# Token mixing over 576 tokens: five tiles of 116 and 112 rows, or four of 128 and a stacked rest of 64

## The chip, the cores and the metric

The program runs on one core of a Trainium2 chip. The core has five engines with a queue of instructions each: PE (TensorE: matmuls and transposes), DVE (VectorE), ACT (ScalarE), POOL (GpSimd) and SP (SyncE), which here issues all loads and stores. Sixteen DMA engines move the data. The metric is device time in microseconds (us), less is better.

## The reference

Three layers follow each other on 4 batches of 576 tokens with 512 channels.

```python
# 1 attention with 8 heads of 64: tokens averaged by 4 (out_up), plus a band |i-j| < 4 (out_local)
attn_out = out_up + out_local
# 2 mixer
xt = x.transpose(0, 2, 1)
h = np.maximum(xt @ w_tok1, 0.0) @ w_tok2        # w_tok1 576x256, w_tok2 256x576
u = x + h.transpose(0, 2, 1)
x = u + np.maximum(u @ w_ch1, 0.0) @ w_ch2       # 512x1536, 1536x512
# 3 four experts of causal attention (head size 64), the best two of a gate weighted and summed
```

The weights of the mixer are float64 in the reference's inputs, so they reach the chip as pairs of 32-bit words and are turned into float32 there.

## The kernel before

**Numbers in two parts.** Products that need float32 accuracy are made from a high and a low part of each operand: `split` writes the high part with ACT and the low part (source minus high) with DVE, and `mm3` adds three matmuls for each pair of tiles, high by high, high by low and low by high.

**First stage, to about 256 us of the profile.** There are 16 units (b, p), one for each batch and pair of heads. `load_qk` and `load_v` issue a unit's loads. `scores` makes the band's scores `sl` and the averaged scores `sd` on PE, their maxima `nmx` and `nd` on DVE, the exponentials `P` (10 instructions) and `Pd` (4) on ACT, the reciprocal sums `rs` and `rd` on DVE, and the products with them on POOL. `turns` transposes them on PE (`pdt` from `Pd`, `tl` from `P`) and ACT copies the results to `PdT` and `PT`. `values` multiplies by the values (`pod`, `ol`) and DVE adds both into `U` (the tile `u`). After each half batch (two units) come three steps of token mixing: `tok_turn` transposes `U` into tiles of tokens (`tx`) and splits them (`xh`, `xl`); `tok_first` multiplies them by the first weight (`h`) and splits the rectified result (`h1h`, `h1l`); `tok_second` multiplies by the second weight (`pu`) and adds to `U`. There are eight half batches. The tokens lie in five tiles, `TS = [116, 116, 116, 116, 112]`.

**The weights.** `tok_weights` loads the first weight in three pieces, `wt_0` and `wt_2` (two tiles of 116 rows each) and `wt_4` (112 rows), then the second in four (`wt_00` to `wt_11`). For each piece `load_f32` puts the load on SP's queue, then two ACT, three DVE and one POOL instruction (`wt_t`, `wt_g`, `wt_a`, `wt_f`), and `split` follows. The order of the first loads is set by `START = 'q0 q1 q2 v0 w v1 v2'`: the token weights come behind the first unit's values. In the same way `convert` turns the channel weights (`wc`, 24 pieces of 512 KB); six of them are turned during the first stage. The raw pieces share two buffers.

**The order of the instructions** on each engine is not the order of the code: a scheduler with a timeline of its own puts them in a row at build time, by priorities (`PRI`, `ahead`) and by what it takes to be ready. Each engine then works through its row strictly, so an instruction that waits holds all behind it. PSUM has four tiles of one bank (`b1`, for `pdt`, `tl`, `pod`, `ol`, `tx`, `h`, `pu`) and two of two banks (`b2`, shared by `sl` and `sd`).

**Second and third stage.** The channel mixing (`c`, some 275 us of PE at work) and the experts (`proj`, `s`, `pt`, `o`, `wo`) follow.

Of the kernel before, what the change touches and what calls it, by code (L numbers as in the profile page):

```python
# [7 lines left out]
F32 = mybir.dt.float32  # L8
F32R = mybir.dt.float32r
# [3 lines left out]
AF = mybir.ActivationFunctionType  # L13
# [3 lines left out]
B, H, S, D = 4, 8, 576, 64  # L17
DM = H * D
NP = 4
TQ = 116  # L20
NT = 5
TS = [TQ, TQ, TQ, TQ, S - 4 * TQ]
WIN, WQ, NW = 64, 58, 10
KS = [min(max(WQ * w - 3, 0), S - WIN) for w in range(NW)]
SD = S // 4
# [2 lines left out]
DT = 256  # L28
# [38 lines left out]
def body(ctx, tc, qT, kT, vw, vp, wt1, wt2, wc1, wc2, wq, wk, wvg, wo, out):  # L67
    nc = tc.nc

    def pool(name, side=None, space=None, stack=ctx):  # L70
        kw = {"side": side} if side else {}
        if space is not None:
            kw["space"] = space
        return stack.enter_context(tc.tile_pool(name=name, bufs=1, reuse_waits="tile", **kw))
# [23 lines left out]
    def behind(ins):  # L98

        if order["on"]:  # L100
            tc.add_manual_dep(ins.ins, order["last"].ins.name,
                              mybir.DependencyInfo(mybir.DependencyClass.NoSync, mybir.DependencyReason.DATA),
                              reason="order")
        order["last"] = ins

    def mm(*a, **kw):
        behind(nc.tensor.matmul(*a, **kw))  # L107

    def tp(*a):
        behind(nc.tensor.transpose(*a))  # L110

    cst = pool("cst")
    ident = cst.tile([128, 128], F32, name="ident")
# [10 lines left out]
    for hf in range(2):  # L124
        m = band[WIN * hf:WIN * hf + WIN]
# [13 lines left out]
    U = [UA[:, :, b * S:(b + 1) * S] for b in range(B)]  # L139

    def split(hi, lo, src, relu=False, scale=None):
        nc.scalar.activation(hi, src, AF.Relu if relu else AF.Copy, **({"scale": scale} if scale else {}))  # L142
        lowpart(lo, src, hi, relu, scale)

    def lowpart(lo, src, hi, relu=False, scale=None):
        h = hi.bitcast(F32)
        if relu:
            nc.vector.scalar_tensor_tensor(lo, src, 0.0, h, op0=OP.max, op1=OP.subtract)  # L148
        elif scale:
            nc.vector.scalar_tensor_tensor(lo, src, scale, h, op0=OP.mult, op1=OP.subtract)  # L150
        else:
            nc.vector.tensor_tensor(lo, src, h, op=OP.subtract)

    def mm3(ps, terms, first=True, last=True):
        n = 3 * len(terms)
        i = 0
        for (lh, ll), (rh, rl) in terms:
            for a, c in ((lh, rh), (lh, rl), (ll, rh)):
                mm(ps, a, c, start=first and i == 0, stop=last and i == n - 1)
                i += 1  # L160

    def flat(t, shape):
        return t.rearrange("p c n -> p (c n)") if len(shape) == 3 else t
# [9 lines left out]
    def load_f32(dram, shape, name, dst=None):  # L173

        P0, n = shape[0], 1
        for d in shape[1:]:
            n *= d
        if dram.dtype == F32:
            if dst is None:
                dst = pv.tile(shape, F32, tag="w64t", bufs=2, name=name + "_t")  # L180
            nc.sync.dma_start(dst, dram)
            return dst
        raw = pv.tile([P0, n, 2], I32, tag="raw64", bufs=2, name=name + "_raw")
        d32 = dram.bitcast(I32)
        if len(shape) == 3:
            nc.sync.dma_start(raw.rearrange("p (c n) t -> p c (n t)", c=shape[1]), d32)
        else:
            nc.sync.dma_start(raw.rearrange("p n t -> p (n t)"), d32)
        h = raw[:, :, 1]
        a = pv.tile([P0, n], I32, tag="w64a", bufs=2, name=name + "_a")  # L190
        f = pv.tile([P0, n], I32, tag="w64f", bufs=2, name=name + "_f")
        g = pv.tile([P0, n], F32, tag="w64g", bufs=2, name=name + "_g")
        t = pv.tile([P0, n], F32, tag="w64t", bufs=2, name=name + "_t")

        nc.scalar.activation(t.bitcast(I32), raw.bitcast(U32)[:, :, 0], AF.Copy, scale=2.0 ** -29)  # L195

        nc.scalar.activation(g, h.bitcast(F32), AF.Abs)

        nc.vector.tensor_scalar(a, h, 3, 0x3FFFFFF8, op0=OP.logical_shift_left, op1=OP.bitwise_and)
        nc.vector.scalar_tensor_tensor(f, h, -0x40000000, a, op0=OP.bitwise_and, op1=OP.bitwise_or)  # L200
        nc.vector.scalar_tensor_tensor(f.bitcast(F32), g, 2.0 ** -15, f.bitcast(F32), op0=OP.is_ge, op1=OP.mult)
        if dst is None:
            dst = t.rearrange("p (c n) -> p c n", c=shape[1]) if len(shape) == 3 else t

        nc.gpsimd.tensor_tensor(flat(dst, shape).bitcast(I32), f, t.bitcast(I32), op=OP.add)  # L205
        return dst
# [10 lines left out]
    pt = pool("pt", side="right", stack=sT)  # L217
# [9 lines left out]
    def tok_split(dram, shape, name):  # L227
        hi = pt.tile(shape, F32R, name=name + "_hi")
        lo = pt.tile(shape, F32R, name=name + "_lo")
        split(flat(hi, shape), flat(lo, shape), flat(load_f32(dram, shape, name), shape))  # L230
        return hi, lo

    tok = {}

    def tok_weights():
        w1 = []
        for t in range(0, NT, 2):
            k = min(2, NT - t)
            m = TS[t] * k
            hi, lo = tok_split(wt1[TQ * t:TQ * t + m].rearrange("(t p) j -> p t j", t=k), [TS[t], k, DT], f"wt1_{t}")  # L240
            w1 += [(hi[:, i], lo[:, i]) for i in range(k)]
        tok["w1"] = w1
        w2 = [[tok_split(wt2[m * 128:(m + 1) * 128, s * HS:(s + 1) * HS], [128, HS], f"wt2_{m}{s}")
               for s in range(2)] for m in range(2)]
        tok["w2"] = w2
# [168 lines left out]
    TK = {}  # L414

    def tok_turn(b, hf):
        xs = []
        for g in range(3):
            ts = [2 * g, 2 * g + 1] if g < 2 else [4]
            tn = TS[ts[0]]  # L420
            ps = b1(f"tx{g}")
            psv = ps.rearrange("p (t d) -> p t d", t=2)
            for i, t in enumerate(ts):
                for j in range(2):
                    tp(psv[:tn, i, j * 128:(j + 1) * 128],
                                        U[b][:, 2 * hf + j, TQ * t:TQ * t + tn], ident)
            hi = pt.tile([TQ, len(ts), 256], F32R, tag=f"xh{g}", bufs=1, name="xh")
            lo = pt.tile([TQ, len(ts), 256], F32R, tag=f"xl{g}", bufs=1, name="xl")
            n = len(ts)
            split(hi[:tn, :n], lo[:tn, :n], psv[:tn, :n])  # L430
            xs += [(hi[:tn, i], lo[:tn, i]) for i in range(n)]
        TK[b, hf] = xs

    def tok_first(b, hf):
        w1, xs = tok["w1"], TK[b, hf]
        ph = b1("h1")
        for m in range(2):
            mm3(ph[:, m * 256:(m + 1) * 256],
                [((w1[t][0][:, m * 128:(m + 1) * 128], w1[t][1][:, m * 128:(m + 1) * 128]), xs[t])
                 for t in range(NT)])  # L440
        hh = pt.tile([128, 2, 256], F32R, tag="h1h", bufs=1, name="h1h")
        hl = pt.tile([128, 2, 256], F32R, tag="h1l", bufs=1, name="h1l")
        split(hh.rearrange("p m d -> p (m d)"), hl.rearrange("p m d -> p (m d)"), ph, relu=True)
        TK[b, hf] = (hh, hl)
# [13 lines left out]
    for what in START.split():  # L458
        if what == "w":
            with ahead("I"):  # L460
                tok_weights()
        else:
            (load_qk if what[0] == "q" else load_v)(*units[int(what[1])])

    n = len(units)
# [20 lines left out]
    def tok_step(i, what):  # L486
        k = i - 2 - DELAY
        if not 0 <= k < n:
            return
        half = (units[k][0], units[k][1] // 2)  # L490
        with ahead(what):
            if what == "K" and k % 2 == 0:
                tok_turn(*half)
            elif what == "F" and k % 2 == 0:
                tok_first(*half)
            elif what == "W" and k % 2 == 1:
                tok_second(*half)
# [102 lines left out]
    for i in range(len(seq) + 1):  # L600
# [10 lines left out]
        g, m = divmod(i, len(blocks))  # L611
# [33 lines left out]
    def v_proj(b, t):  # L645

        ts = slice(t * TQ, t * TQ + TS[t])
        ps = b1("vp")
        mm3(ps[:TS[t], :260], [((x[0][:, ts], x[1][:, ts]), WV[c]) for c, x in enumerate(ST[b]["xs"])])
        nc.scalar.activation(ST[b]["VV"][:TS[t], t], ps[:TS[t], :256], AF.Copy)  # L650
        nc.vector.tensor_copy(ST[b]["L"][:TS[t], t], ps[:TS[t], 256:260])
# [162 lines left out]
    for i, (b, p) in enumerate(pairs):  # L814
# [11 lines left out]
        last = nxt is None  # L826
# [99 lines left out]
```

## Time and profile before

| what | us |
|---|---|
| median of three runs | 749.37 |
| lowest and highest of them | 747.67, 752.47 |
| span of the profiled execution, first to last instruction | 747.5 |

The runs' list gives no time of its own for the profiled execution beside its span; the median run is 1.9 us longer than the span. PE works 685.1 us of the span. A change is worth what it moves the end of the last instruction; work that an engine does beside a busy PE costs nothing.

### The profile page before, as it was taken

The page shows a single profiled execution, that of the slowest core. Times are in us where ns is not written, and L with a number is a line of the kernel's source. Part 1 is how long each engine was busy: PE and PEld are TensorE (multiplying, and loading weights), DVE is VectorE, ACT ScalarE, POOL GpSimd, SP SyncE. Part 2 cuts the span into 40 slices and gives each one's busy share as a digit, 9 for nine tenths or more (in the row PEclk, how much of TensorE's full clock was granted, in tenths as well). Part 3 has the DMA queues.
Part 4 walks back from the last instruction along what each step waited for, and adds up shares of the span by engine and source line. Part 5 has one row for each costly group of instructions (what it writes and reads, how often), then busy time and mean ns, then how long its engine had stood idle before and what let it go on. Part 6 is the DMA issues. An engine that isn't in the chain of part 4 may idle for free.

```text
span 747.5 us, 13362 instructions
## 1 busy us (share of the span) xinstructions
PE 685.1 (92%) x4908; PEld 594.4 (80%) x4908; DVE 469.6 (63%) x1076; ACT 387.8 (52%) x1235; POOL 164.7 (22%) x196
## 2 busy tenths in 40 slices
PE   4176979999999999999999999999997999999987
PEld 3154767787889988888888898888896988889875
DVE  4587798556545596874575455444258777777773
ACT  5458586665643465432443233222247676686674
POOL 4477796444300131120100000000213030010000
PEclk9568889999999999999999999999999999999999
DMA  8777765342100141120101010000020122021102
GB/s 221 188 209 225 221 200 167 95 136 59 36 2 1 37 133 57 29 84 1 51 7 57 1 29 14 15 1 0 1 61 12 25 61 61 15 90 33 33 29 100
DMA packets 31737, 52.26 MB, mean 70 GB/s; under 512 B 3704, under 2 KB 16504, under 8 KB 31672
## 3 DMA queue, kind: packets, MB, share of 16 engines
q1 hardware_dynamic: 31672, 51.40, 23.7%
q8 instruction: 39, 0.64, 0.4%
q14 instruction: 26, 0.21, 0.1%
HBM read 41.95 MB, written 4.72 MB: 62 GB/s over the span
## 4 chain that ended last, share of the span: by engine, by line
PE 80%; DVE 8%; DMA 6%; ACT 3%; SPq 2%; issue 1%; POOL 0%; ACTq 0%; DVEq 0%
PE c L107 40%; PE proj L107 6%; PE vp L107 4%; PE s L107 4%; PE h L107 4%; PE o L107 4%; PE wo L107 3%; PE pu L107 3%; PE sl L107 3%; PE pt L110 3%; PE ol L107 2%; DMA vz<-in_vw_dram 2%; DMA wc_raw<-in_wc_dram 2%; PE pod L107 1%; PE tl L110 1%; PE sd L107 1%
## 5 line engine op out<-in xcount | busy, mean ns | idle before, releaser
L107 PE MATMUL c<-hh,wcl 128*128 128x460 f32 (+1 forms) x240 | 89.3, 372 | 0.0
L107 PE MATMUL c<-uh,wcl 128*128 128x460 f32 (+1 forms) x240 | 89.3, 372 | 0.0
L107 PE MATMUL c<-ul,wch 128*128 128x460 f32 (+1 forms) x240 | 89.2, 372 | 0.0
L107 PE MATMUL c<-hh,wch 128*128 128x460 f32 (+1 forms) x240 | 89.2, 372 | 0.0
L107 PE MATMUL c<-hl,wch 128*128 128x460 f32 (+1 forms) x240 | 89.2, 372 | 0.0
L107 PE MATMUL c<-uh,wch 128*128 128x460 f32 (+1 forms) x240 | 89.1, 373 | 0.0
L142 ACT ACTIVATE hh<-c 128x460 fp32r<-128x460 f32 (+1 forms) x60 | 33.1, 551 | 100.4 <-PE c L107 99.8
L148 DVE SCALAR_TENSOR_TENSOR hl<-c,hh 128x460 fp32r<-128x460 f32 (+1 forms) x60 | 38.1, 635 | 53.8 <-ACT hh L142 53.7
L205 POOL TENSOR_TENSOR wc_t<-wc_f,wc_t 128x512 int32<-128x512 int32 x24 | 33.9, 1418 | 165.9 <-ACT wc_t L195 149.2
L532 ACT ACTIVATE uh<-u 128x460 fp32r<-128x460 f32 (+1 forms) x80 | 46.2, 586 | 34.4 <-PE c L107 25.2
L339 ACT ACTIVATE P<-sl,nmx 128x64 f32<-128x64 f32 x160 | 48.2, 332 | 17.3 <-DVE nmx L333 17.2
L533 DVE TENSOR_TENSOR ul<-u,uh 128x460 fp32r<-128x460 f32 (+1 forms) x80 | 49.8, 634 | 11.5 <-ACT uh L532 11.5
L728 ACT ACTIVATE Pc<-s,nm 112x576 f32<-112x576 f32 (+4 forms) x80 | 44.4, 559 | 16.0 <-DVE nm L725 15.8
L107 PEld LDWEIGHTS c<-hl,wch 128*128 128x128 f32 x240 | 45.3, 189 | 5.2
L107 PEld LDWEIGHTS c<-uh,wcl 128*128 128x128 f32 x240 | 45.2, 188 | 5.3
L107 PEld LDWEIGHTS c<-ul,wch 128*128 128x128 f32 x240 | 45.2, 188 | 5.1
L107 PEld LDWEIGHTS c<-hh,wch 128*128 128x128 f32 x240 | 45.1, 188 | 5.0
L107 PEld LDWEIGHTS c<-uh,wch 128*128 128x128 f32 x240 | 45.1, 188 | 5.0
L107 PEld LDWEIGHTS c<-hh,wcl 128*128 128x128 f32 x240 | 45.2, 188 | 4.9
L725 DVE TENSOR_REDUCE nm<-s 112x1 f32<-112x576 f32 (+4 forms) x80 | 40.5, 514 | 11.7 <-PE s L107 10.2
L107 PE MATMUL s<-K,Q 128*112 128x288 f32 (+3 forms) x192 | 42.7, 320 | 3.5 <-DVE Q L150 1.8
L731 DVE TENSOR_SCALAR Pc<-Pc,su,gw 112x576 f32<-112x576 f32 (+4 forms) x80 | 38.4, 481 | 2.3
(170 smaller groups left out, 1759.4 us busy)
## 6 DMA issues: line engine op xcount, KB each, us to landing
wc_raw<-in_wc_dram SPq DMA_DIRECT2D x24, 512.0 KB, 4.1
vp<-in_vp_dram SPq DMA_DIRECT2D x16, 336.0 KB, 3.5
vz<-in_vw_dram SPq DMA_DIRECT2D x32, 160.0 KB, 4.2
qT<-in_qT_dram SPq DMA_DIRECT2D x16, 288.0 KB, 4.1
kz<-in_kT_dram SPq DMA_DIRECT2D x32, 144.0 KB, 3.9
kT<-in_kT_dram SPq DMA_DIRECT2D x16, 288.0 KB, 5.3
K<-K SPq DMA_DIRECT2D x64, 72.0 KB, 2.0
out_dram<-y SPq DMA_DIRECT2D x18, 256.0 KB, 2.0
```

The lines of the kernel that those rows point to most:

```text
L107: behind(nc.tensor.matmul(*a, **kw))
L110: behind(nc.tensor.transpose(*a))
L142: nc.scalar.activation(hi, src, AF.Relu if relu else AF.Copy, **({"scale": scale} if scale else {}))
L148: nc.vector.scalar_tensor_tensor(lo, src, 0.0, h, op0=OP.max, op1=OP.subtract)
L205: nc.gpsimd.tensor_tensor(flat(dst, shape).bitcast(I32), f, t.bitcast(I32), op=OP.add)
L339: nc.scalar.activation(P[:, t, h], sv[:, bk, i], AF.Exp, bias=nmx[:, bk, i:i + 1], scale=0.125, accum_out=sm[:, t, h:h + 1])
L532: nc.scalar.activation(hi, u, AF.Copy)
L533: getattr(nc, ULO).tensor_tensor(lo, u, hi.bitcast(F32), op=OP.subtract)
L725: nc.vector.tensor_reduce(nm[:nq], sv, axis=AX.X if t < 4 else AX.XY, op=OP.max, negate=True)
L728: nc.scalar.activation(pv_, sv, AF.Exp, bias=nm[:nq], accum_out=su[:nq])
L731: nc.vector.tensor_scalar(P[:nq, :n], P[:nq, :n], su[:nq], ST[b]["W"][:nq, t, 2 * p + e:2 * p + e + 1], op0=OP.mult, op1=OP.mult)
```

## The change

The tokens of the mixing are cut into four tiles of 128 and a rest of 64 (`REM`). The first weight is loaded in two pieces of 2 x 128 rows and one of 64. The rest's high and low parts are stacked: `xr` (name `both`) holds the high part of the 64 tokens in rows 0 to 63 and the low part in rows 64 to 127; `wt_rh` holds the weight's high part twice, `wt_rl` its low part above zeros. Two matmuls with `xr` then stand for the three of `mm3`. `tok_second` and everything after it are as before.

```diff
-        for t in range(0, NT, 2):
-            k = min(2, NT - t)
-            m = TS[t] * k
-            hi, lo = tok_split(wt1[TQ * t:TQ * t + m].rearrange("(t p) j -> p t j", t=k), [TS[t], k, DT], f"wt1_{t}")
-            w1 += [(hi[:, i], lo[:, i]) for i in range(k)]
-        tok["w1"] = w1
+        for t in range(0, 4, 2):
+            hi, lo = tok_split(wt1[128 * t:128 * t + 256].rearrange("(t p) j -> p t j", t=2), [128, 2, DT], f"wt1_{t}")
+            w1 += [(hi[:, i], lo[:, i]) for i in range(2)]
+        wr = [pt.tile([128, DT], F32R, name=f"wt1_r{x}") for x in "hl"]
+        nc.gpsimd.memset(wr[1][REM:].bitcast(F32), 0.0)
+        src = load_f32(wt1[512:S], [REM, DT], "wt1_4")
+        split(wr[0][:REM], wr[1][:REM], src)
+        nc.scalar.activation(wr[0][REM:], src, AF.Copy)
+        tok["w1"] = w1, wr
...
-            tn = TS[ts[0]]
+            tn = 128 if g < 2 else REM
...
-            hi = pt.tile([TQ, len(ts), 256], F32R, tag=f"xh{g}", bufs=1, name="xh")
-            lo = pt.tile([TQ, len(ts), 256], F32R, tag=f"xl{g}", bufs=1, name="xl")
+            if g == 2:
+                both = pt.tile([128, 256], F32R, tag="xr", bufs=1, name="xr")
+                split(both[:REM], both[REM:], psv[:REM, 0])
+                continue
+            hi = pt.tile([128, 2, 256], F32R, tag=f"xh{g}", bufs=1, name="xh")
+            lo = pt.tile([128, 2, 256], F32R, tag=f"xl{g}", bufs=1, name="xl")
...
         for m in range(2):
-            mm3(ph[:, m * 256:(m + 1) * 256],
-                [((w1[t][0][:, m * 128:(m + 1) * 128], w1[t][1][:, m * 128:(m + 1) * 128]), xs[t])
-                 for t in range(NT)])
+            ms = slice(m * 128, (m + 1) * 128)
+            o = ph[:, m * 256:(m + 1) * 256]
+            mm3(o, [((w1[t][0][:, ms], w1[t][1][:, ms]), xs[t]) for t in range(4)], last=False)
+            for i, w in enumerate(wr):
+                mm(o, w[:, ms], both, start=False, stop=i == 1)
```

The scheduler makes a new order of the whole first stage from this. Three places matter. Line numbers shift by one to four in the changed kernel.

On DVE, at the program's start, the row of the kernel before from the sums of unit 0 (`rs`, `rd`) to the first two pieces of the token weight:

```order
L342 TENSOR_SCALAR rs<-sm 128x10
L343 RECIPROCAL rs<-rs 128x10
L199 TENSOR_SCALAR wt_0_a<-wt_0_raw 116x512
L200 SCALAR_TENSOR_TENSOR wt_0_f<-wt_0_raw,wt_0_a 116x512
L362 TENSOR_SCALAR rd<-sdm 72x4
L199 TENSOR_SCALAR wt_2_a<-wt_2_raw 116x512
L363 RECIPROCAL rd<-rd 72x4
L200 SCALAR_TENSOR_TENSOR wt_2_f<-wt_2_raw,wt_2_a 116x512
```

The same place on DVE in the changed kernel:

```order
L346 TENSOR_SCALAR rs<-sm 128x10
L347 RECIPROCAL rs<-rs 128x10
L200 TENSOR_SCALAR wt_0_a<-wt_0_raw 128x512
L201 SCALAR_TENSOR_TENSOR wt_0_f<-wt_0_raw,wt_0_a 128x512
L366 TENSOR_SCALAR rd<-sdm 72x4
L367 RECIPROCAL rd<-rd 72x4
L200 TENSOR_SCALAR wt_2_a<-wt_2_raw 128x512
L201 SCALAR_TENSOR_TENSOR wt_2_f<-wt_2_raw,wt_2_a 128x512
```

The reciprocal of unit 0's `rd` stood behind the first instruction on `wt_2` and now stands ahead of it; both kernels have all of it behind `wt_0`.

On PE, ahead of the transposes `pdt` and `tl` of unit 4 (its `P` is named `P_0_820`), in the kernel before; `qT_2_863` is the query of unit 6:

```order
L107 MATMUL ol<-PT_3_751,vz_108 64x54 x2
L107 LDWEIGHTS identb
L107 MATMUL sl<-band,identb 128x320
L107 LDWEIGHTS identb
L107 MATMUL sl<-band,identb 128x320
L107 MATMUL sl<-kz_105,qT_2_863 64x128 x3
L110 MATMUL pdt<-ident,Pd 112x72 x4
L110 MATMUL pdt<-ident,Pd 96x72 x2
L107 MATMUL sl<-kz_105,qT_2_863 64x128
L107 MATMUL sl<-kz_105,qT_2_863 64x64 x3
L110 MATMUL tl<-ident,P_0_820 128x128 x3
```

On PE, the same transposes of unit 4 (`P_0_819`) in the changed kernel; `qT_1_682` is the query of unit 5:

```order
L108 MATMUL ol<-PT_3_752,vz_108 64x54
L108 MATMUL sl<-kz_107,qT_1_682 64x128 x4
L108 MATMUL sl<-kz_107,qT_1_682 64x64 x4
L108 MATMUL sl<-kz_107,qT_1_682 64x128 x4
L108 MATMUL sd<-kd,qd 72x144 x4
L111 MATMUL pdt<-ident,Pd 112x72 x4
L111 MATMUL pdt<-ident,Pd 96x72 x2
L111 MATMUL tl<-ident,P_0_819 128x128 x5
```

The scores stood two units ahead of the transposes there and now stand one unit ahead. So it is in both orders from the transposes of unit 3 on, to the last scores.

On ACT, from unit 4's copy `PT_0` on, in the kernel before; `P_2` are the exponentials of unit 6, and `h1h` and `wc` belong to the mixing and to the channel weights:

```order
L385 ACTIVATE PT_0_909<-tl 128x384
L195 ACTIVATE wc_0_t<-wc_0_raw 128x512
L385 ACTIVATE PT_0_909<-tl 128x256
L339 ACTIVATE P_2_1186,sm<-sl,nmx 128x64 x10
L359 ACTIVATE Pd,sdm<-sd,nd 72x144 x4
L397 ACTIVATE OdT<-pod 128x144
L142 ACTIVATE wch_426<-wc_2_t 128x512
L197 ACTIVATE wc_1_g<-wc_1_raw 128x512
L197 ACTIVATE wc_2_g<-wc_2_raw 128x512
```

On ACT, the same place in the changed kernel; `P_1` are the exponentials of unit 5, whose transposes come next on PE:

```order
L389 ACTIVATE PT_0_908<-tl 128x384
L198 ACTIVATE wc_3_g<-wc_3_raw 128x512
L389 ACTIVATE PT_0_908<-tl 128x256
L343 ACTIVATE P_1_988,sm<-sl,nmx 128x64 x10
L363 ACTIVATE Pd,sdm<-sd,nd 72x144 x4
L401 ACTIVATE OdT<-pod 128x144
L143 ACTIVATE wch_432<-wc_1_t 128x512
L198 ACTIVATE wc_4_g<-wc_4_raw 128x512
```

Between unit 4's copies and unit 5's the exponentials were those of unit 6 and are now those of unit 5, and the channel weights are further on: `wc_3` of the first matrix stands where `wc_0` of the second stood, three pieces before it.

## Rows read from the trace of the kernel before

**Rows 1.** The page: engines' busy time, then PE in 40 slices

```profile
PE 685.1 (92%) x4908; PEld 594.4 (80%) x4908; DVE 469.6 (63%) x1076; ACT 387.8 (52%) x1235; POOL 164.7 (22%) x196
...
PE   4176979999999999999999999999997999999987
```

**Rows 2.** Windows by stage: start:end, length, busy of five engines, clock, DMA share, GB/s

```profile
30.00:60.00 30.00, 19.00 (x194) 14.20 (x194) 25.87 (x51) 20.57 (x103) 21.37 (x27) 0.64 0.83 222
60.00:130.00 70.00, 57.70 (x612) 46.10 (x610) 57.04 (x113) 49.55 (x209) 54.28 (x60) 0.88 0.69 203
130.00:225.00 95.00, 94.52 (x1036) 76.85 (x1033) 51.88 (x121) 56.55 (x265) 32.88 (x45) 1.00 0.23 66
```

**Rows 3.** PE in order of time at the start: start us, length, instruction, idle before

```profile
17.30 0.80 PE L107 MATMUL sd<-kd,qd 64*72 64x144 f32 x8
29.79 0.97 PE L110 MATMUL pdt<-ident,Pd 72*112 72x72 f32 x6 [11.69 <-POOL Pd L364]
...
35.98 0.69 PE L107 MATMUL sl<-band,identb 128*128 128x320 bf16 x2 [4.15 <-ACT P L339]
```

**Rows 4.** POOL and ACT in order of time, 28 to 33 us

```profile
28.23 1.50 POOL L364 TENSOR_TENSOR Pd<-Pd,rd 72x576 f32<-72x576 f32 x1 [10.43 <-DVE rd L363]
...
32.35 0.31 ACT L339 ACTIVATE P<-sl,nmx 128x64 f32<-128x64 f32 x1
```

**Rows 5.** DVE in order of time, 14 to 28 us

```profile
14.72 0.56 DVE L271 TENSOR_TENSOR vp<-vp 112x384 f32<-112x384 f32 x1 [2.78 <-DMA vp<-in_vp_dram]
...
22.09 0.43 DVE L199 TENSOR_SCALAR wt_a<-wt_raw 116x512 int32<-116x512 int32 x1 [6.48 <-DMA wt_raw<-in_wt_dram]
...
23.16 0.16 DVE L362 TENSOR_SCALAR rd<-sdm 72x4 f32<-72x4 f32 x1
27.58 0.43 DVE L199 TENSOR_SCALAR wt_a<-wt_raw 116x512 int32<-116x512 int32 x1 [4.26 <-DMA wt_raw<-in_wt_dram]
27.92 0.17 DVE L363 RECIPROCAL rd<-rd 72x4 f32<-72x4 f32 x1
```

**Rows 6.** SP's queue in order of time, 9 to 28 us

```profile
9.33 1.17 SPq L186 DMA_DIRECT2D wt_raw<-in_wt_dram  x2
10.68 6.42 SPq L265 DMA_DIRECT2D vz<-in_vw_dram  x4
...
22.08 5.96 SPq L287 DMA_DIRECT2D kz<-in_kT_dram  x2
```

**Rows 7.** Windows within the start, columns as in rows 2

```profile
2.00:14.00 12.00, 4.32 (x34) 3.10 (x35) 5.90 (x12) 7.27 (x28) 4.84 (x15) 1.00 0.97 278
14.00:16.00 2.00, 1.70 (x14) 1.19 (x15) 0.86 (x3) 1.65 (x10) 0.65 (x2) 1.00 0.28 93
16.00:22.00 6.00, 2.10 (x26) 1.51 (x23) 0.00 (x0) 0.00 (x0) 1.65 (x3) 0.91 1.00 214
22.00:30.00 8.00, 0.21 (x2) 0.21 (x3) 3.62 (x7) 2.48 (x4) 1.50 (x1) 0.50 0.39 121
24.00:28.00 4.00, 0.00 (x0) 0.00 (x0) 0.42 (x2) 0.42 (x1) 0.00 (x0) 0.50 0.26 91
30.00:46.00 16.00, 9.84 (x100) 7.89 (x99) 14.40 (x23) 8.68 (x40) 13.24 (x16) 0.61 1.01 265
```

**Rows 8.** PE in order of time, two matmuls of `h` in a dense stretch

```profile
157.00 0.28 PE L107 MATMUL h<-xh,wt_lo 112*128 112x256 f32 x1
157.12 0.28 PE L107 MATMUL h<-xh,wt_hi 116*128 116x256 f32 x1
```

**Rows 9.** From unit 11's scores to its product, and PE's transposes of units 9 and 10

```profile
153.02 0.59 PE L110 MATMUL pdt<-ident,Pd 72*112 72x72 f32 x6
...
153.13 0.82 DVE L332 TENSOR_REDUCE nmx<-sl 128x10 f32<-128x640 f32 x1
...
162.05 1.14 POOL L364 TENSOR_TENSOR Pd<-Pd,rd 72x576 f32<-72x576 f32 x1
...
162.79 0.59 PE L110 MATMUL pdt<-ident,Pd 72*112 72x72 f32 x6
```

More of the change, by code (lines that the diff above doesn't have):

```diff
@@ L22 @@
 TS = [TQ, TQ, TQ, TQ, S - 4 * TQ]
+REM = S - 512
 WIN, WQ, NW = 64, 58, 10
@@ L425, in tok_turn @@
                     tp(psv[:tn, i, j * 128:(j + 1) * 128],
-                                        U[b][:, 2 * hf + j, TQ * t:TQ * t + tn], ident)
-            hi = pt.tile([TQ, len(ts), 256], F32R, tag=f"xh{g}", bufs=1, name="xh")
-            lo = pt.tile([TQ, len(ts), 256], F32R, tag=f"xl{g}", bufs=1, name="xl")
[L429 to L432, printed above, removed]
+                                        U[b][:, 2 * hf + j, 128 * t:128 * t + tn], ident)
+            if g == 2:
[4 more added lines that the diff above has]
+            lo = pt.tile([128, 2, 256], F32R, tag=f"xl{g}", bufs=1, name="xl")
+            split(hi, lo, psv)
+            xs += [(hi[:, i], lo[:, i]) for i in range(2)]
+        TK[b, hf] = xs, both
     def tok_first(b, hf):
-        w1, xs = tok["w1"], TK[b, hf]
+        (w1, wr), (xs, both) = tok["w1"], TK[b, hf]
         ph = b1("h1")
         for m in range(2):
-            mm3(ph[:, m * 256:(m + 1) * 256],
-                [((w1[t][0][:, m * 128:(m + 1) * 128], w1[t][1][:, m * 128:(m + 1) * 128]), xs[t])
-                 for t in range(NT)])
+            ms = slice(m * 128, (m + 1) * 128)
[3 more added lines that the diff above has]
+                mm(o, w[:, ms], both, start=False, stop=i == 1)
         hh = pt.tile([128, 2, 256], F32R, tag="h1h", bufs=1, name="h1h")
```

## The prediction, made before the changed kernel ran

> **What bounds the kernel now.** I read the page first. PE works 92% of the span, and its slices are full but for the first eight or so, some 150 us [rows 1]. So a change in the token mixing can gain in two ways: by less PE work where PE is full, and by less idle time at the start. The windows by stage say where the border lies: in 130 to 225 us PE works 94.5 of 95 us at full clock, in 60 to 130 only 57.7 of 70, in 30 to 60 only 19.0 of 30 [rows 2]. In 60 to 130 nothing is at its limit: DVE works 57.0, POOL 54.3, DMA 0.69 of the time [rows 2]. The engines wait for each other there, so whatever comes earlier at the start moves all of it, until PE is full; from there the end follows PE.
>
> Then I read PE in order of time at the start. The reader should see one hole of 11.69 us, between unit 1's scores and unit 0's transposes, which wait for POOL's product `Pd`; 4.15 us more are lost ahead of unit 2's scores, waiting for ACT's `P` [rows 3]. POOL had itself waited 10.43 us for DVE's `rd`, and `P` of unit 1 began on ACT only at 32.35 [rows 4]. On DVE the cause stands in the row: it waits 6.48 us for `wt_0`'s load, to 22.09, and 4.26 us for `wt_2`'s, to 27.58; `rd` and its reciprocal stand behind these two waits, though what they need was there before [rows 5]. The first token weights are not wanted before the first half batch, but DVE takes its row in turn.
>
> Why do these two loads land so late? They were issued from 9.33 [rows 6], behind loads of which the last, `vp`, had landed at 14.72 [rows 5]. While those ran, DMA was busy 0.97 of the time at 278 GB/s. Then the share falls to 0.28 (14 to 16 us) and, after a stretch at 1.00, to 0.26 in 24 to 28 us, at 91 GB/s [rows 7]. 0.26 of sixteen engines is 4.2: four engines work and twelve have nothing. Meanwhile SP needs 6.42 us to issue four loads and 5.96 for two [rows 6], so the queue behind is held as well.
>
> **The change part by part.** *The loads.* The pieces of 116 rows become pieces of 128, 512 KB instead of 464 each, and the third piece becomes smaller. The unchanged loads of 128 rows for `qT` and `kT` make up much of the stretch with a share of 0.97 [rows 7], so I take it that a load of 128 rows uses all engines. 524 KB take 1.9 us at 278 GB/s and 2.45 us at the 214 GB/s of 16 to 22 us [rows 7]. From 14.72, `wt_0` then lands at 16.6 to 17.2 and `wt_2` at 18.5 to 19.6, that is 8.0 to 9.1 us before 27.58.
>
> By the Trainium skill (DMA: Bandwidth & Descriptors, "Why a DMA increments its semaphore by 16 and not by 1") a load runs on the largest number of engines up to 16 that divides its row count: 4 for 116, 16 for 128, 112 and 64; the share of 0.26 agrees. By the row alone, the twelve engines might also idle because SP was held; then 128 rows would gain nothing here, and the term below would be 0.
>
> What follows these landings: `rd`'s reciprocal no longer stands behind `wt_2`, so unit 0's transposes can start some 10 us earlier: 1.07 us from `wt_0`'s first instruction to `rd` [rows 5], 0.2 for the reciprocal, 1.5 for POOL [rows 4], about 20 instead of 29.79 [rows 3]. But unit 2's scores decide what comes next; they wait for `P` of unit 1, whose maxima stand behind `wt_2` on DVE, so they gain `wt_2`'s 8.0 to 9.1 us. DMA bounds this from the other side. The capacity wasted is 0.72 x 2 + 0.61 x 8 = 6.3 us of all engines, and from 30 to 46 us the share is 1.01 [rows 7]: loads there can come only 6.3 us earlier, while the engines could come 8 to 9 earlier. So the lead is 6.3 to 9.1 us; I take **7.5**, about the middle, since both limits act in turn.
>
> *The matmuls.* Each half batch has 2 x 2 for the rest where it had 2 x 3, so 2 fewer of 30, 16 in all. In a dense stretch the next starts 0.12 us after the last, for 112 and for 116 rows alike [rows 8]: 1.9 us at most. The first two half batches fall before 130 us, where PE is not full; 12 matmuls count, **1.4 us**. The lower bound is 0.
>
> *Small things.* One more ACT copy and one more memset, once, in the start; the splits and transposes keep their number and their columns. The rest's low part must now be whole before its first matmul, where only the third needed it last: DVE has it long before, as the rest stands at the end of `h`'s first half. I take 0 for all this; half a microsecond either way is in the range.
>
> *The order.* It moved more than the change asked for: scores one unit ahead of their transposes instead of two. That adds a wait on PE. Unit 11's scores ended by 153.1 and its `Pd` was ready at 163.19 [rows 9], so this chain through DVE, ACT, DVE and POOL took 10.1 us, with half a unit's worth of other work in it. PE, meanwhile, took 9.77 us from unit 9's transposes to unit 10's, one unit of work [rows 9], 9.5 without the two matmuls. With one unit between, PE lacks up to 0.6 us. A unit's chain spans the wait ahead of the unit before as well as its own, so the two share the 0.6: 0.3 a unit, over the units 8 to 15 some 2.4 us. The lower bound is 0, since the chain holds waits of its own that shrink when its unit is the next one wanted. I take **1.5 us** lost. Behind a waiting `pdt` stand `tl`, `h` or `pu`, `pod`, `ol`; DVE waits for these with `u`, SP with the loads into `vz`.
>
> In 60 to 130 us the order does two opposite things: it takes a unit's scores out of PE's way and the channel weights into ACT's and DVE's. I found no row that prices this; its bounds are the stage's own slack, 12.3 us of idle PE [rows 2], to the good, and as much to the bad. I take 0.
>
> The granted clock was 0.50 at 22 to 30 us and 0.61 to 46, behind PE's hole [rows 3, 7], the lower level (1.2 GHz) for most of it. A smaller hole may bring it back earlier. PE is not what is waited for there, so I add nothing.
>
> *Sum.* 747.5 of span, less 7.5, less 1.4, plus 1.5, is 740.1; the median of the runs lies 1.9 above the profiled span, which makes **742.0**, with 733 to 751 about it.
>
> **The rivals.** *The lead is spent on the way* (744 to 749). Where ACT carries three more pieces of channel weights by unit 5, its row waits for their loads too, and the half batches behind come no earlier than now. For it: DVE works 57.0 of 70 us in that stage and gets this work sooner. Against: the same work is missing later, and the order in which units finish is kept. Spending 3 to 7 of the 7.4 us leaves 745 to 749. Nearly the same time comes if 128 rows load no faster: then only 1.4 is left and 1.5 lost, 749.
>
> *Slower: the shorter lead of the scores.* The place is `pdt` on PE, units 3 to 14. In the stage to 130 us the chain of 10.1 us has channel weights in ACT's row and a loaded DVE in it. If it takes 12.5 us against 9.5 of PE work, neighbouring waits add up to 3 and each of 12 units loses 1.5: 18 us, less the 8.9 gained, is 9 us slower, 758. It outweighs the gain from a chain of 11.0 us on (0.75 us a unit).
>
> *Faster still.* With the loads early and the weights turned early, the middle stage closes its 12.3 us of idle PE as well. Half of it more gives 736.
>
> **How the numbers follow.** Two kernels here can be told apart at about 1%, 7.5 us. The forecast (738 to 744) has 0.41, the further gain (below 738) 0.20, the lead spent or the loads unchanged 0.29, slower 0.10. The limit of 1% lies at 741.9, in the middle of the forecast: faster by over 1% gets 0.20 and 0.25 of the forecast's 0.41, so 0.45; slower by over 1% 0.08; the rest, 0.47, is within 1%. The range reaches to 733 and 751, which leaves a tenth out at each end.
>
> **What would show it.** In the changed kernel's profile: DMA's share stays near 1 from 2 to 40 us with no stretch at 0.26; DVE's waits for the token weight are under 3 us together and end before 20; PE's hole ahead of unit 0's `pdt` falls from 11.69 to 2 or 3 us; unit 2's scores start at 27 to 30 us; PE is full some 7 us before 130. In 130 to 225 us small waits of `pdt` for POOL's `Pd` appear, under 3 us in sum. `h` has 224 matmuls instead of 240. I am wrong if the share stays at 0.26, if the lead is there at 50 us and gone at 130, or if the waits of `pdt` pass 9 us.

## The result, and the profile after

The changed kernel took 742.6 us (median of four runs, 741.68 to 743.38); the kernel before, beside it, 750.1. The ratio is 0.990, with an interval of 0.9875 to 0.9925. Its profiled execution spans 741.4 us and took 743.14. In a later run on another chip it took 741.4 against 749.9 (ratio 0.9893).

The page of the changed kernel, the rows that answer [rows 1]:

```profile
PE 680.7 (92%) x4892; PEld 593.2 (80%) x4892; DVE 478.1 (64%) x1076; ACT 387.5 (52%) x1236; POOL 162.5 (22%) x197
...
PE   3468889889999999999999999999998999999987
```

TensorE has 16 matmuls fewer and is busy for 4.4 us less; the second slice is fuller (4 for 1), but slices 8 and 9 are no longer full. The windows by stage (start:end, length, busy of PE, PEld, DVE, ACT and POOL, clock, DMA share, GB/s) answer [rows 2]:

```profile
30.00:60.00 30.00, 20.21 (x216) 15.31 (x214) 27.06 (x48) 21.54 (x94) 22.42 (x29) 0.67 0.85 247
60.00:130.00 70.00, 62.35 (x654) 50.60 (x651) 59.32 (x109) 46.34 (x196) 46.98 (x56) 0.88 0.59 170
130.00:225.00 95.00, 87.90 (x975) 74.05 (x972) 51.77 (x118) 53.55 (x259) 30.17 (x41) 0.98 0.22 62
```

From 60 to 130 us PE works 62.35 us where it worked 57.70; from 130 to 225, where it was full with 94.52, it works 87.90. The second number was not forecast. At the start the same columns answer [rows 7]:

```profile
14.00:16.00 2.00, 0.80 (x4) 0.28 (x5) 0.00 (x0) 2.00 (x14) 1.08 (x2) 0.50 1.04 258
...
24.00:28.00 4.00, 0.00 (x0) 0.00 (x0) 3.96 (x8) 3.78 (x21) 3.29 (x4) 0.50 1.06 287
```

The two stretches with a share of 0.28 and 0.26 are gone: the DMA engines now move 258 and 287 GB/s there, where it was 93 and 91. DVE in order of time (start, length, instruction, idle before and what ended it) answers [rows 5]:

```profile
16.37 0.56 DVE L275 TENSOR_TENSOR vp<-vp 112x384 f32<-112x384 f32 x1 [3.53 <-DMA vp<-in_vp_dram]
17.58 0.44 DVE L200 TENSOR_SCALAR wt_a<-wt_raw 128x512 int32<-128x512 int32 x1 [0.32 <-DMA wt_raw<-in_wt_dram]
...
20.20 0.43 DVE L200 TENSOR_SCALAR wt_a<-wt_raw 128x512 int32<-128x512 int32 x1
```

PE in order of time answers [rows 3]:

```profile
21.69 0.97 PE L111 MATMUL pdt<-ident,Pd 72*112 72x72 f32 x6 [2.79 <-POOL Pd L368]
...
28.79 0.69 PE L108 MATMUL sl<-band,identb 128*128 128x320 bf16 x2 [5.07 <-ACT P L343]
```

DVE waits 0.32 us for the token weight where it waited 6.48 and 4.26. Unit 0's transposes start at 21.69 instead of 29.79, unit 2's scores at 28.79 instead of 35.98: 7.2 us of lead. From there the lead can be followed by the first `pod` of each unit: 7.2 us at unit 0 (31.59 against 38.79), 7.9 at unit 7 (126.11 against 134.01), 6.0 at unit 15 (213.55 against 219.51), 6.1 at the end of the span.

What PE lacks behind 130 us stands in the chain of work that the end waited for (start, length, what):

```profile
129.14 1.19 PE sl L108 x19
130.34 4.78 DMA qT<-in_qT_dram
135.15 0.75 DVE qd L306
135.90 0.38 DVE u L464
136.32 1.89 PE pu L108 x12
```

This is a wait that the prediction had elsewhere. `qT` has three buffers; with scores one unit ahead, the load into the next one goes out only when the scores that read it end (129.14 + 1.19 is 130.33). The average `qd` waits for this load, and DVE takes its row in turn: behind `qd` stand the sums `u` of the mixing, and PE's `pu` waits for them. The same happens at 154.94. PE's waits from 130 to 225 us (what waits, for what: us in all, times, longest), where the kernel before has 0.4 us in all:

```profile
PE pu L108 <- DVE u L464: 3.8, 2, 2.2
PE pu L108 <- ACT PdT L383: 3.0, 4, 1.2
```

There is no wait of `pdt` for `Pd` among them. And the second hole has a further price, seen in PE's rows in order of time:

```profile
160.57 0.40 PE L108 MATMUL pu<-wt_hi,h1h 128*128 128x288 f32 x1 [2.22 <-DVE u L464]
...
161.32 0.34 PE L108 MATMUL pu<-wt_hi,h1l 128*128 128x288 f32 x1
161.46 0.44 PE L108 MATMUL pu<-wt_hi,h1h 128*128 128x288 f32 x1
161.70 0.44 PE L108 MATMUL pu<-wt_lo,h1h 128*128 128x288 f32 x1
```

and in the window around them, columns as above:

```profile
160.00:165.00 5.00, 4.43 (x22) 3.22 (x22) 2.57 (x9) 1.37 (x8) 2.02 (x3) 0.66 0.01 3
```

After 2.22 us without work PE starts its matmuls 0.13 us apart, and from 161.46 on 0.24 apart: the granted clock is at its lower level for most of these 5 us (0.66 of full speed on the mean, so about 3.4 us at 0.50). In the kernel before it was 1.00 through this whole stage [rows 2].

### The profile page after: what moved, and what is told of

It is laid out like the page before. It is cut to its first block, busy times and chain, and to the rows that moved or that the text cites. A ratio compares the mean times of both kernels' runs of the same rounds, so it can differ in the third digit from the quotient of the medians.

```text
span 741.4 us, 13335 instructions
## 1 busy us (share of the span) xinstructions
PE 680.7 (92%) x4892; PEld 593.2 (80%) x4892; DVE 478.1 (64%) x1076; ACT 387.5 (52%) x1236; POOL 162.5 (22%) x197
## 4 chain that ended last, share of the span: by engine, by line
PE 81%; DVE 8%; ACT 4%; DMA 3%; POOL 1%; issue 1%; SPq 0%; ACTq 0%; POOLq 0%; DVEq 0%
PE c L108 41%; PE proj L108 7%; PE vp L108 4%; PE s L108 4%; PE o L108 4%; PE h L108 3%; PE wo L108 3%; PE ol L108 3%; PE pu L108 3%; PE sl L108 3%; PE pt L111 3%; DMA qT<-in_qT_dram 2%; PE pod L108 2%; PE tx L111 1%; ACT P L343 1%
```

## The experiments

Three theories. **Loads**: 116 rows occupy four DMA engines, and this alone is the gain. **Matmuls**: stacking saves 1.4 to 1.9 us. **Order**: scores one unit ahead cost the time lost behind 130 us. Their rival throughout is that the order which the scheduler makes anew for each kernel, not the edit, sets the time. All runs, with PE's busy time in two stages (the ratio is formed over the rounds, and is not the quotient of the medians shown):

| run | median us | ratio to before (interval) | PE 60 to 130 | PE 130 to 225 |
|---|---|---|---|---|
| kernel before | 749.9 to 751.1 | 1 | 57.70 | 94.52 |
| changed kernel | 742.6 | 0.990 (0.9875 to 0.9925) | 62.35 | 87.90 |
| tiles116_load112p4 | 742.3 | 0.9911 (0.9893 to 0.9929) | 59.70 | 94.76 |
| tiles116_load92p24 | 746.7 | 0.9963 (0.9951 to 0.9975) | 58.89 | 94.77 |
| tiles128_load116p12 | 755.4 | 1.0100 (1.0062 to 1.0137) | 49.93 | 92.67 |
| tiles128_load112p16 | 749.0 | 0.9982 (0.9961 to 1.0004) | 55.56 | 92.06 |
| tiles128_rest_unstacked | 751.6 | 0.9995 (0.9964 to 1.0026) | 62.27 | 88.42 |
| tiles128_four_queries | 751.0 | 0.9982 (0.9961 to 1.0003) | 52.28 | 93.33 |
| tiles128_scores_two_ahead | 746.1 | 0.9925 (0.9900 to 0.9950) | 54.65 | 94.76 |
| tiles116_weights_last | 753.9 | 1.0029 (1.0006 to 1.0053) | 53.49 | 94.76 |
| tiles128_control | 741.4 | 0.9893 (0.9863 to 0.9923) | 59.36 | 87.86 |
| tiles128_unstacked_again | 751.9 | 1.0025 (0.9999 to 1.0051) | 61.01 | 89.13 |
| tiles128_three_raw | 738.3 | 0.9850 (0.9819 to 0.9881) | 57.26 | 94.18 |
| tiles128_two_ahead_three_raw | 746.9 | 0.9954 (0.9933 to 0.9975) | 52.09 | 94.83 |

**The loads alone.** The kernel before, its tiles and its 240 matmuls of `h` kept, with each of the first two token weight loads cut in two: 112 and 4 rows, or 92 and 24 (the diff shows the first). The two kernels have the same instructions in the same order on every engine.

```diff
-        if len(shape) == 3:
+        if len(shape) == 3 and P0 == 116:
+            rv = raw.rearrange("p (c n) t -> p c (n t)", c=shape[1])
+            for r in (slice(0, 112), slice(112, P0)):
+                nc.sync.dma_start(rv[r], d32[r])
+        elif len(shape) == 3:
             nc.sync.dma_start(raw.rearrange("p (c n) t -> p c (n t)", c=shape[1]), d32)
```

> The kernel before, with each of the first two token-weight loads issued as two: rows 0 to 111 and rows 112 to 115. Tiles, matmuls and sums are those of before; the scheduler made a new order, the same as for the run with rows 0 to 91 and 92 to 115. Theory A (the gain of the change comes from these two loads, which ran on 4 of 16 DMA engines): the DMA share stays near 1 to 25 us, the wait of DVE for the token weight falls from 10.7 us to under 4, and the time is 6 to 8 us under the kernel before, 742 to 744. Theory B (the gain comes from 16 fewer matmuls and the new order): no gain, 748 to 751.

> The same edit with the cut at row 92: 92 rows, whose largest divisor up to 16 is 4, and 24 rows. The order of all instructions is that of the run with 112 and 4 rows, so only the loads differ. Theory A: 368 of 464 KB of each piece still run on 4 engines, so most of the hole comes back: a share near 0.25 for some 4 to 6 us and a time 4 to 6 us above the run with 112 and 4 rows. Theory B: the two runs agree within 1 us.

The first gained 7.7 us, as much as the whole change; the second is 4.3 us behind it. As the extra issues made the scheduler move other instructions too, against the kernel before, only these 4.3 us are free of the order: they are the price of the difference between 92 + 24 and 112 + 4 rows. The 3.4 us from 116 rows to 92 + 24 may hold both the loads and the order. The window from 24 to 28 us, with 112 + 4 rows:

```profile
24.00:28.00 4.00, 1.75 (x11) 1.48 (x10) 4.00 (x4) 0.63 (x1) 3.71 (x3) 1.00 1.06 232
```

Its start of unit 0's transposes, in PE's order of time:

```profile
23.71 0.97 PE L110 MATMUL pdt<-ident,Pd 72*112 72x72 f32 x6 [4.14 <-POOL Pd L368]
```

The same window with 92 + 24, and its second half:

```profile
24.00:28.00 4.00, 0.00 (x0) 0.00 (x0) 0.06 (x1) 0.07 (x1) 0.00 (x0) 0.50 0.46 125
26.00:28.00 2.00, 0.00 (x0) 0.00 (x0) 0.06 (x1) 0.07 (x1) 0.00 (x0) 0.50 0.26 85
```

and its start of unit 0's transposes:

```profile
30.15 0.97 PE L110 MATMUL pdt<-ident,Pd 72*112 72x72 f32 x6 [10.93 <-POOL Pd L368]
```

Only the number of rows in a load differs, and the share is 1.06 or 0.46, from 26 to 28 us 0.26, as with 116 rows. By the Trainium skill (DMA: Bandwidth & Descriptors, "Why a DMA increments its semaphore by 16 and not by 1") 112 rows run on 16 engines and 92 on 4; the shares of 1.06 and 0.26 agree. The prediction had left open that the twelve engines idle because SP is held. The pair shows it the other way round: the same four issues of the token weight take SP twice as long with 92 + 24 rows. First with 112 + 4, then with 92 + 24:

```profile
10.10 2.60 SPq L188 DMA_DIRECT2D wt_raw<-in_wt_dram  x4
9.88 5.29 SPq L188 DMA_DIRECT2D wt_raw<-in_wt_dram  x4
```

**The new tiles with old loads.** The changed kernel, its loads of 128 rows cut into 116 and 12 or 112 and 16 by the same edit; again both have the same order on every engine.

> The changed kernel, with each of its first two token-weight loads issued as two: rows 0 to 115 and rows 116 to 127. Tiles, stacking and matmuls are those of the changed kernel; the scheduler made a new order, with the scores two units ahead of their transposes. Theory A: 116 rows on 4 engines bring back the hole: DMA share about 0.25 in two stretches, PE's wait ahead of unit 0's transposes near 10 us, and 6 to 8 us above the run with 112 and 16 rows. Theory B: as that run, within 1 us.

> The same with the cut at row 112: 112 and 16 rows. Its order is that of the run with 116 and 12 rows on all engines, so the pair differs only in the loads; against the changed kernel it differs in the order, scores two units ahead instead of one. Theory A for the pair: 6 to 8 us under its twin. On the order: if one unit ahead is what cost PE the 7 us of idle time in 130 to 225 us, PE is full there again and the time is 736 to 740; if that loss is made up elsewhere anyway, it is that of the changed kernel, 742 to 744.

The pair differs by 6.4 us, as the loads theory has it; the hole ahead of unit 0's transposes is 6.46 us with 116 + 12 rows, not near 10, and the larger one, 11.20, comes ahead of unit 2's scores. But the order of this pair has the scores two units ahead, and its better half took 749.0, outside both expected ranges and 6.4 us more than the changed kernel with the same use of the engines. So two units ahead is not enough for a better order, as one reading of the loss behind 130 us had suggested; what this order wins there (92.06 us of PE for 87.90) it loses between 60 and 130 (55.56 for 62.35), where PE stood still once for 7.19 us:

```profile
65.72 1.59 PE L111 MATMUL tx<-ident,u 128*128 128x128 f32 x6 [7.19 <-ACT OdT L405]
```

ACT has that `OdT` in its row behind a piece of channel weights, ahead of which it waited 4.21 us for DVE's `wt_lo`, and behind eight of a unit's ten exponentials.

**The wait in DVE's row without faster loads.** The kernel before with `START = 'q0 q1 q2 v0 v1 v2 w'`.

> The kernel before, with its pieces of 116 rows, but the token weights put at the end of the list of first loads, behind the values of units 1 and 2; on VectorE the sums of unit 0 and their reciprocal then stand ahead of the first token weight. If VectorE's wait in its row is all that costs: the hole ahead of unit 0's transposes falls to about 3 us and the time to 742 to 744, as with loads on sixteen engines. If the idle DMA engines cost by themselves (6.3 us of capacity, still lost as the share falls to 0.26 somewhere before 40 us): the hole is gone, but loads behind come as late as before and the time is 747 to 750.

Unit 0's `rd` now stands ahead of the token weights, and the hole at `pdt` falls to 1.52 us; PE in order of time:

```profile
20.95 0.59 PE L110 MATMUL pdt<-ident,Pd 72*112 72x72 f32 x6 [1.52 <-POOL Pd L364]
...
35.83 0.69 PE L107 MATMUL sl<-band,identb 128*128 128x320 bf16 x2 [13.75 <-ACT P L339]
```

and DVE:

```profile
25.67 0.43 DVE L199 TENSOR_SCALAR wt_a<-wt_raw 116x512 int32<-116x512 int32 x1 [7.64 <-DMA wt_raw<-in_wt_dram]
...
26.74 0.82 DVE L332 TENSOR_REDUCE nmx<-sl 128x10 f32<-128x640 f32 x1
...
31.08 0.43 DVE L199 TENSOR_SCALAR wt_a<-wt_raw 116x512 int32<-116x512 int32 x1 [2.92 <-DMA wt_raw<-in_wt_dram]
31.43 0.17 DVE L333 TENSOR_SCALAR nmx<-nmx 128x10 f32<-128x10 f32 x1
```

The wait only went one unit on: now the first instruction of unit 1's `nmx` stands behind `wt_0`, and the second behind `wt_2`, whose load is there at 31.08. This second wait ends last: unit 1's exponentials start on ACT at 32.20, and unit 2's scores come at 35.83, where they came at 35.98 [rows 3]. The time is 753.9, no better than before and above both expected ranges. The hole at `pdt` was the visible loss, but the scores behind it set the time. As the loads still have 116 rows (the share is 0.26 again from 30 to 32 us), the run does not part the wait in DVE's row from the slow loads.

**Four buffers for the queries.** The changed kernel with `bufs=4` for `qT`.

> The changed kernel with four buffers for the queries instead of three; scores still one unit ahead, only a few rows of the order move. If the 7 us that TensorE loses in 130 to 225 us come from the average of the next query, which waits in VectorE's row for a late load and holds the sums into U behind it: that load goes out a unit earlier, the waits of the second product for these sums fall from 3.8 us to under 1, TensorE works over 91 of the 95 us instead of 87.9, and the time falls by 2 to 5 us to 738 to 741. If the shorter lead of the scores itself is the cause (the chain to the product on GpSimd too long): the time stays at 742 to 743 and the waits only change their name.

Behind 130 us the theory holds: no wait of `pu` for `u` is left, its waits for `PdT` fall from 3.0 to 1.2 us, and PE works 93.33 of 95. The time does not follow: 751.0 is outside both expected ranges. The query's loads now stand ahead of the channel weights' on SP, and ACT waits for these with unit 3's exponentials behind them in its row. One of these waits, in ACT's order of time:

```profile
61.48 0.68 ACT L198 ACTIVATE wc_g<-wc_raw 128x512 f32<-128x512 f32 x1 [3.39 <-DMA wc_raw<-in_wc_dram]
```

PE, where it waits in turn (`pdt` waits twice for `Pd` in this stage, 10.0 us together):

```profile
67.62 0.69 PE L108 MATMUL sl<-band,identb 128*128 128x320 bf16 x2 [3.69 <-ACT P L343]
...
75.98 0.97 PE L111 MATMUL pdt<-ident,Pd 72*112 72x72 f32 x6 [4.11 <-POOL Pd L368]
```

**Scores two ahead with loads of 128 rows.** `PRI` for `S` 60 instead of 30.

> The changed kernel with the scheduler's priority for scores raised from 30 to 60, which brings back the order of the kernel before, scores two units ahead of their transposes, with the loads of 128 rows. If one unit of lead costs the 7 us: 735 to 738. If the order two units ahead is no better with this start (as the run with pieces of 112 and 16 rows suggests): 742 to 749, with what is won in 130 to 225 us lost in 60 to 130.

746.1, in the second range: 94.76 us of PE behind 130 us, as in the kernel before, and 54.65 of 70 ahead of it. Over all runs the loss behind 130 us goes with the lead of the scores and the query's buffers: with scores one unit ahead and three buffers PE works 87.86 to 89.13 us there, with a fourth buffer 93.33, and in all runs with scores about two units or more ahead there 92.06 to 94.83.

**The rest without stacking.** The changed kernel with three matmuls on 64 rows for each output.

```diff
-                split(both[:REM], both[REM:], psv[:REM, 0])
+                split(both[0], both[1], psv[:REM, 0])
...
-            for i, w in enumerate(wr):
-                mm(o, w[:, ms], both, start=False, stop=i == 1)
+            (wh, wl), (xh, xl) = wr, both
+            for i, (a, c) in enumerate(((wh, xh), (wh, xl), (wl, xh))):
+                mm(o, a[:, ms], c, start=False, stop=i == 2)
```

> The changed kernel with the rest of 64 tokens not stacked: three matmuls on 64 rows instead of two on 128 (240 matmuls of h instead of 224), no copy of the high part, no zeroed rows. Loads and, but for some rows, the order stay. Stacking worth its matmuls: 1.4 to 1.9 us slower than the changed kernel, about 744.3. Stacking worth nothing (mixing beside other work): within 0.5 us, 742.1 to 743.1. If the stacking were the main cause of the gain: 748 or more.

> The changed kernel itself, unaltered, beside the next run on the same chip, because the times of the unstacked rest were spread over more than 10 us there. Every theory expects 742 to 743 as before; if this one is spread as widely, the spread belongs to that chip and not to the stacking.

> The same kernel as the unstacked rest before (three matmuls on 64 rows instead of two on 128), a second time. Stacking worth its matmuls: 1.4 to 1.9 us above the control in this job. The row of VectorE or ScalarE in the first stage worse by the few lines that moved: 4 us or more above it, with TensorE's loss seen between 130 and 225 us, as the first profile had it (unit 15's values at 216.3 instead of 213.6).

10.5 us slower than the control on the same chip, where the matmuls saved account for 1.9 at most. Both runs lie where they were expected if stacking were the main cause of the gain, but they do not show that, as matmuls on 64 rows bring a cost of their own. TensorE's rows tell most of it. In the changed kernel, from the last matmul of the fourth tile over the rest to the next output:

```profile
147.92 0.28 PE L108 MATMUL h<-xh,wt_lo 128*128 128x256 f32 x1
148.04 0.28 PE L108 MATMUL h<-xr,wt_rh 128*128 128x256 f32 x1
...
148.28 0.28 PE L108 MATMUL h<-xh,wt_hi 128*128 128x256 f32 x1
```

and unstacked, in the second of the two runs:

```profile
152.97 0.28 PE L108 MATMUL h<-xh,wt_lo 128*128 128x256 f32 x1
153.18 0.50 PE L108 MATMUL h<-xr,wt_hi 64*128 64x256 f32 x2
153.52 0.28 PE L108 MATMUL h<-xr,wt_lo 64*128 64x256 f32 x1
153.73 0.38 PE L108 MATMUL h<-xh,wt_hi 128*128 128x256 f32 x1
153.95 0.28 PE L108 MATMUL h<-xl,wt_hi 128*128 128x256 f32 x1
```

Stacked, the passage takes 0.36 us, three steps of 0.12. Unstacked it takes 0.76, 0.28 more than four such steps: 0.21 on going from 128 rows to 64, 0.34 for the two (0.22 and 0.12), 0.21 on going back; and the first step after the return is 0.22 too. So each change lengthens two steps. A dense half batch of `h` takes 4.13 us from its first to its last start instead of 3.32; eight would cost 6.5 us (an estimate, 1.9 of it the 16 matmuls more). The kernel before did not pay this: between its tiles of 116 and 112 rows the step is 0.12 [rows 8]. The Trainium skill (TensorEngine Tiling (Array Packing), "Tiling Modes") lists 64 rows as another tiling mode than 128 and says that changing the mode drains TensorE; the steps of 0.21 agree, if a plain matmul on 64 rows is such a mode. The remaining 4 us are not settled: this kernel's order has a few moved rows too, and its times spread over 10 us (747.75 to 758.24) where the control's spread over 6.5.

**Three buffers for the raw weights.** `bufs=3` for `raw64`, in the changed kernel and in the one with scores two ahead.

> The changed kernel with three buffers for the raw pieces of weights instead of two; the scheduler then puts scores two units ahead again and the channel weights later on ScalarE. If what holds the stage from 60 to 130 us are waits for the channel weights' loads in the rows of VectorE and ScalarE: these waits fall under 2 us together, TensorE works more than 62.4 of the 70 us there and nearly all of the 95 behind, 734 to 739. If the stage is held by the chain of scores and products itself: TensorE works 55 to 60 of the 70 us and the time is 742 to 749.

> Both edits, the scores' priority of 60 and three raw buffers. With the priority alone VectorE waited 14.3 us and ScalarE 7.6 us for loads of channel weights between 30 and 130 us, and TensorE worked 54.7 of 70 us. If these waits are the cause: under 3 us together, TensorE works over 60 of the 70 us, and the time falls by 4 to 8 us against the priority alone. If not: the same time within 2 us.

The first is the fastest of all, 1.5% under the kernel before and 3.1 us under the control (their intervals just overlap). Its scores stand two units or more ahead of the transposes from unit 4 to unit 13, so that lead alone is not what made the other orders slow. From 30 to 130 us neither ACT nor DVE waits for a channel weight there (4.8 us for token weights), and behind 130 PE works 94.18 of 95 us, with unit 15's values at 205.35 instead of the control's 216.01. But from 60 to 130 it works 57.26, not over 62.4, so the reason given did not hold as stated. The second run speaks against it too: 746.9, no better than the priority alone, though DVE's waits for channel weights fell from 14.3 to 2.0 us. ACT's only fell from 7.6 to 6.6, so this test is a half one. These loads are not shown to be what holds the middle stage.

## Why the prediction was right

**The loads** were its main term and right in mechanism, and near in size: 7.5 us forecast, 7.2 of lead at unit 0's values and unit 2's scores. How much of such a lead reaches the end is less sure. Free of the order, the two cuts differ by 4.3 us in the old tiles and 6.4 in the new ones, where unit 2's scores lie 6.4 and 9.1 us apart in the profiles (31.42 and 37.85, 30.64 and 39.70); the 7.7 of 112 + 4 rows has a new order in it. As forecast, the hole at `pdt` fell to 2.79 us, unit 2's scores began between 27 and 30, and the DMA share stayed at its limit up to 30 us (behind that it was 0.82 to 46, not 1). The rival in which 128 rows load no faster is refuted by these shares, and the 92-row pieces show that the row count makes them.

**The matmuls** were right by the rows: from its first to its last start a half batch of `h` takes 3.32 us (146.52 to 149.84), in the kernel before 3.56 (155.25 to 158.81), two steps of 0.12 less. That is 1.9 us for eight half batches, of which 1.4 were counted. No run isolates this saving, since undoing the stacking brings 64 rows and their switches with it. Unstacked, the new tiling loses all that the loads gain, in part by that switch.

**The order** was right in sum and wrong in place, and this is the step that failed. It put 1.5 us on `pdt` waiting for `Pd` behind 130 us; there is no such wait. Instead PE worked 6.6 us less in that stage (94.52 to 87.90): 3.8 us of waiting at `pu` behind `u`, `qd` and a late `qT`, and 3.0 at `pu` behind `PdT`, of which the fourth buffer took 1.8 away and the rest was not followed. The prediction had followed the chain of the scores to POOL, and not what else a shorter lead moves: the load that waits for the scores' buffer, and on DVE what stands behind the instruction that waits for that load. (In the kernel before the scores are two units ahead throughout from unit 9 to unit 13; ahead of the transposes of units 6 and 8 it is only about one.)

**The stage from 60 to 130 us**, taken as 0 with bounds of 12.3 either way, gave 4.65 us more of PE at work. With the 6.6 lost behind it that is 2.0 us net, close to the 1.5 forecast, because two errors cancelled: that is luck. It is not the order's price either, since the busy time of a window is not the work done in it: the lead fell by only 1.9 us from unit 7 to unit 15. By the leads the order cost some 3 us, an estimate: 7.2 at the start and 1.9 of matmuls make 9.1, of which 6.1 is left. All of this gain is there when the first stage ends, as the start of its last `pu` shows, in the kernel before and in the changed one:

```profile
255.85 0.30 PE L107 MATMUL pu<-wt_hi,h1l 128*128 128x288 f32 x1
249.66 0.30 PE L108 MATMUL pu<-wt_hi,h1l 128*128 128x288 f32 x1
```

Of the 6.1 us PE is idle for 1.7 less and busy for 4.4 less; the 16 matmuls are 1.9 of that, and the other 2.5 stay open. The runs show how far this could have gone: with engines fully used and 128 rows, orders that the scheduler made from small edits lie between 738.3 and 751.0. Where these orders lose their time is known for single waits only; which of the moved instructions make the stage from 60 to 130 us long or short stays open.

**The clock** was given no term. In the kernel before it was at the upper level from 115 to 225 us; in the changed one the hole of 2.22 us ahead of 160.57 was followed by matmuls at nearly twice the distance. For these 12 `pu` it cost 0.6 us (2.53 instead of 1.89), and for the six `pod` behind them 0.6 more (1.46 at 163.10, 0.84 at 138.21). None of that is idle time, so it comes on top of the waits.

**The forecast sign that PE is full 7 us before 130** did not appear, for the reason given under the order; the slower rival (waits at `pdt` over 12 units) did not occur either, and the lead was not spent ahead of 130 us (7.9 us at unit 7).

## What to carry to other kernels

When a load's stretch shows a DMA share near a quarter while the queue is full, look at its row count first: cutting 116 rows into 112 and 4, with the order that the scheduler made of it, gained as much here as retiling the whole mixing. Before a matmul on 64 rows is put among others of 128, look at the step at the switch, and stack the parts to full height if the rows of 64 come often. And where a scheduler makes the order, price what each moved instruction holds on its own engine and which buffer it frees, not just the chain that it belongs to; repeat an edit's control on the same chip before calling a few us its effect.

## What the runs showed of the hardware

- Where matmuls on 64 rows stand among ones on 128, each change lengthens two steps, to 0.21 and 0.22 us from 0.12; from 116 to 112 rows the step stays 0.12.
- Loads of 92 and 116 rows leave the DMA engines at a share of 0.26 for stretches (26 to 28 us with 92 + 24, 24 to 28 with 116); with 112 + 4 and 128 rows it is 1.06 from 24 to 28 us. The same instructions in the same order then differ by 4.3 and 6.4 us of the whole time.
- The queue that issues feels it as well: the same four issues of the token weight took SP 5.29 us with 92 + 24 rows and 2.60 with 112 + 4, 6.52 with 116 + 12 and 2.62 with 112 + 16.
- A wait of TensorE of 2.22 us was followed by matmuls 0.24 us apart instead of 0.13, at a granted clock of 0.66 over 5 us; one of 1.61 us (ahead of 136.32) was not, at 1.00.
